# Sliding-window attention inside an MLP, one core: the scores and PVs of two head pairs issued as one group from batch 2 on

## The chip, the core and the metric

The kernel runs on one core of a Trainium2 chip. The metric is the device time of one execution in microseconds (us); the number compared is the median over several executions.

The engines have short names here, as in the profile: PE is TensorE (matmuls; PEld is its weight load), ACT is ScalarE, DVE is VectorE, POOL is GpSimd, SP is SyncE, which here only issues DMAs ("SPq" is its queue, "ACTq" is ACT issuing a DMA). Matmuls write to PSUM, which has eight banks; ACT and DVE read PSUM and write to SBUF.

## What is computed

Cut to what matters, the reference is:

```python
# q, k, v: [8 batches, 8 heads, 576 positions, 64]; w_in: [512, 2048]; w_out: [2048, 512]
scores = q @ k.T / 8                      # per batch and head
mask   = (0 <= i - j) & (i - j < 64)      # each query sees itself and the 63 keys before it
attn   = softmax(where(mask, scores, -1e9))
x      = (attn @ v), heads side by side   # [4608 tokens, 512]
h      = x @ w_in
out    = (h * clip(h + 3, 0, 6) / 6) @ w_out
```

The inputs are float32 and the kernel computes in bf16 with float32 accumulation. Most of the arithmetic is in the two products with `w_in` and `w_out`; the attention only needs a band of 64 keys per query.

## The kernel before

**The two-product part.** The 4608 tokens are cut into nine blocks T of 512. For each block, `s1(T)` (L747) computes the hidden layer in eight chunks c of 2 x 128 features: each chunk is eight matmuls of 512 columns (L767) into one PSUM slot, a RELU by ACT (L776) and a multiply by DVE (L779), which frees the slot and writes `gT`. Then `s2(T)` (L787) multiplies `gT` by `w_out`: 4 x 16 matmuls of 512 columns (L815), numbered n = 0 to 63, into two accumulator banks; after every 16th, `finish` (L825) has ACT copy the result to SBUF (L832) and SP store it (L837).

**The attention part** of batch b = T + 1 is woven into `s2(T)`, because `s1(T + 1)` needs its result. Eight heads are four pairs g. One pair's work is a unit "S" (scores) and a unit "PV":

- From batch 2 on (`NR6 = 2`), S is `scores64` (L637). A head's 576 queries are nine blocks i of 64. For each block and each head h of the pair, one matmul (L648) multiplies the block's 64 queries by a window of 128 keys (`kwin`, L627); it uses half of the PE's rows. Two parts, of five and four blocks, go to a PSUM slot each; ACT takes the exponential of a slot in one instruction (`ex`, L654), into the tile `pT`, 1152 columns per pair; after the second part DVE multiplies all of them by a 0/1 mask in place (`msk`, L658).
- PV is `pv64` (L665): 20 matmuls (L672) with `pT` as weights and V (or its copy shifted by 64 keys, `W`) as moving operand, half of the PE's columns each, into one PSUM slot. A column of ones in V gives the sums of the softmax. Then `norm` (L708) on DVE takes the reciprocals (L710) and multiplies (L713) into `opg`, and `xdma` (L717) has SP issue a DMA transpose of `opg` into `xT` (L720), the input of `s1`.

**What these wait for.** The queries and keys of a batch come in by SP (L455, ten DMAs a batch), are cast by POOL (`nat`, L277), and are transposed into `QKT` by two DMA transposes on SP's queue (L434, four pairs each). There is one `QKT` buffer (`NQT = 1`), so the next batch's transposes follow this batch's last scores. V comes in by DMAs that ACT issues (L381) and is cast by POOL. A ring of four tiles `P_ring` (`NPT = 4`, L193) holds `pT`; a pair takes tile (4b + g) mod 4.

**PSUM.** From `s2(0)` on there are three slots of two banks each and two accumulator banks. `two_banks` (L160) gives out the slot that comes free first and waits until its readers are done: a chunk's multiply, a part's exponential, or a pair's `norm`.

**The order of the work** is fixed when the program is built. `Plan` (L36) keeps a time of its own for the PE (`pl.t`), with a cost for each step; every operation of another engine has a due time and a cost, and on each engine they are put in order of due time (`pop`, L59). So the planner's costs decide the order in an engine's queue, and on the chip each queue is then worked off in that order. Where the attention units stand among the 64 matmuls of `s2` is written by hand: `REST` (L879) lists pairs of (n, unit). For batches 2 to 7, before: S of pair 0 ahead of matmul n = 4, S of pair 1 ahead of 10, S of pair 2 and PV of pair 0 ahead of 17, S of pair 3 and PV of pair 1 ahead of 23, PV of pair 2 ahead of 28, PV of pair 3 ahead of 33. Batches 0 and 1 use `FIRST`, `scores` and `pv128` (L573, L679).

Of the kernel before, what the change touches and what calls it, by code (L numbers as in the profile page):

```python
# [12 lines left out]
EXP = mybir.ActivationFunctionType.Exp  # L13
RELU = mybir.ActivationFunctionType.Relu
MULT = mybir.AluOpType.mult
# [7 lines left out]
NPT = 4  # L23
# [81 lines left out]
def kernel(  # L105
# [10 lines left out]
    P = nc.NUM_PARTITIONS  # L116
    B, H, S, D = q.shape
    DM, FF = moe_w_in.shape
    NT = B * S
    NG = H // 2  # L120
# [12 lines left out]
    scale = 1.0 / math.sqrt(D)  # L133
# [4 lines left out]
    pl = Plan()  # L138
# [15 lines left out]
    def free_at(i):  # L154
        return max((pl.done.get(r, 1e9) for r in held[i]), default=0.0)
# [4 lines left out]
    def two_banks(readers, dt=F32):  # L160
        i = min(range(len(psums)), key=free_at)
        while free_at(i) >= 1e9:
            pl.pop()
            i = min(range(len(psums)), key=free_at)
        for r in held[i]:
            pl.wait(r)
        held[i] = readers
        return psums[i].tile([P, 2, 512 if dt == F32 else 1024], dt, name=f"ps{i}", tag="ps")
# [10 lines left out]
    mask = consts.tile([P, QW], BF16, name="mask")  # L179
# [9 lines left out]
    def qk(b, i, g):  # L189

        return QK_tiles[b % NQT][:, 2 * g + i if b < NR6 else i * NG + g, :]

    P_ring = [consts.tile([P, 2, KB, 2 * P], BF16, name=f"pT{i}") for i in range(NPT)]  # L193
    V_ring = [consts.tile([P, NG, KB, 2, VW], BF16, name=f"V{i}") for i in range(2)]
    runs_flat = runs_all[:].rearrange("p a b c d -> p (a b c d)")
    NV = NG * KB * 2 * VW
    W_ring = [runs_flat[:, i * NV : (i + 1) * NV].rearrange("p (g k h w) -> p g k h w", g=NG, k=KB, h=2) for i in range(2)]
    BL = S // D

    mask64 = consts.tile([P, D], BF16, name="mask64")  # L200
# [14 lines left out]
    for j, t in enumerate(P_ring):  # L215
        at("ACT", 1.9, 0.55, lambda t=t: nc.scalar.copy(
            out=t[:, :, 0 : KB - 1, QW : 2 * P], in_=idle[:].rearrange("p (h k w) -> p h k w", h=2, w=D)))
        at("DVE", 2.0, 0.1, lambda t=t: nc.vector.memset(t[:, :, KB - 1, D:QW], 1.0))

    def band(t, fill):  # L220
# [12 lines left out]
        out=neg[:, 0 : 2 * QW].rearrange("p (k w) -> p k w", k=2),  # L233
        in_=neg32[:].unsqueeze(1).to_broadcast([P, 2, QW]),
    ) and None, None, deps=("neg32",))
    pl.op("DVE", 4.4, 0.25, lambda s: nc.vector.tensor_copy(
        out=neg[:, 2 * QW : 2 * QW + D], in_=neg32[:, 0:D]) and None, "neg", deps=("neg32",))
# [5 lines left out]
        out=m64[:], in_=m64[:], pattern=[[1, D]], compare_op=ISGE, fill=0.0, base=D, channel_multiplier=-1))  # L243
    at("POOL", 17.4, 0.3, lambda: nc.gpsimd.affine_select(
        out=m64[:], in_=m64[:], pattern=[[-1, D]], compare_op=ISGE, fill=0.0, base=-1, channel_multiplier=1), "m64")
# [381 lines left out]
    def kwin(b, g, i, h):  # L627

        t = QK_tiles[b % NQT]
        c = (2 * g + 1 if b < NR6 else NG + g) * SP + (i - 1) * D  # L630
        return t[:].rearrange("p a s -> p (a s)")[h * D : (h + 1) * D, c : c + P]

    def blocks(b, g):
        n = b * NG + g
        return P_ring[n % NPT][:].rearrange("p h k w -> p (h k w)")[:, 0 : 2 * S].rearrange("p (h c) -> p h c", h=2)

    def scores64(b, g):  # L637

        for i in range(2):
            pl.wait(("tr", b, i))  # L640
        QT, pT = qk(b, 0, g), blocks(b, g)
        for part in range(2):
            i0, i1 = ((0, 5), (5, BL))[part]
            st = two_banks([("exp", b, g, part)])
            for i in range(i0, i1):
                for h in range(2):
                    c = (i - i0) * D
                    nc.tensor.matmul(  # L648
                        st[:, h, c : c + D], lhsT=kwin(b, g, i, h), rhs=QT[h * D : (h + 1) * D, i * D : (i + 1) * D],
                        start=True, stop=True,  # L650
                    )
            pl.pe((0.25, 0.22)[part])
            def ex(s, st=st, i0=i0, i1=i1):
                nc.scalar.activation(  # L654
                    out=pT[:, :, i0 * D : i1 * D], in_=st[:, :, 0 : (i1 - i0) * D], func=EXP, scale=scale,
                )
            def msk(t):
                pl.op("DVE", t, 0.8, lambda s: nc.vector.tensor_tensor(  # L658
                    out=pT.rearrange("p h (i w) -> p (h i) w", w=D), in0=pT.rearrange("p h (i w) -> p (h i) w", w=D),
                    in1=mask64[:].unsqueeze(1).to_broadcast([P, 2 * BL, D]), op=MULT,  # L660
                ) and None, ("mask", b, g), deps=("mask64",))
            pl.op("ACT", pl.t + 0.1, (0.8, 0.69)[part], ex, ("exp", b, g, part), msk if part else None)
        pl.mark(("S", b, g), pl.t)

    def pv64(b, g, o):  # L665

        V, W, pT = V_ring[b % 2], W_ring[b % 2], blocks(b, g)
        for h in range(2):
            for m in range(KB):
                for odd in range(2):  # L670
                    i = min(2 * m + odd, BL - 1)
                    nc.tensor.matmul(  # L672
                        o[odd * D : (odd + 1) * D, h, m * VW : (m + 1) * VW],
                        lhsT=pT[:, h, i * D : (i + 1) * D],
                        rhs=(V if i % 2 else W)[:, g, m, h, :], start=True, stop=True,
                    )
        pl.pe(0.5)
# [18 lines left out]
    def pv(b, g):  # L696
# [3 lines left out]
        if b >= NR6:  # L700
            pl.need(("w0", b % 2))
            pv64(b, g, o)
        else:
            pv128(b, g, o)
# [82 lines left out]
    def s2(T, side):  # L787

        side = list(side)
        if T == 0:  # L790
            order = [(ts, fc) for f0 in (0, 8, 12) for ts in (0, 1) for fc in range(f0, 8 if f0 == 0 else f0 + 4)]
            order += [(ts, fc) for ts in (2, 3) for fc in range(NFC)]
        else:
            order = [(ts, fc) for ts in range(TB // P) for fc in range(NFC)]
        last = T == NTB - 1
        order = [(ts, 0, DM, fc) for ts, fc in order if not last or ts < TB // P - 1]
        if last:
            order += [(TB // P - 1, c0, c1, fc) for c0, c1 in ((0, 3 * P), (3 * P, DM)) for fc in range(NFC)]
        accs = {}
        for n, (ts, c0, c1, fc) in enumerate(order):  # L800
            while side and side[0][0] <= n:
                at_, f, b, g = side[0]
                if b < NR6 and not ready(f, b, g):
                    break
                side.pop(0)
                unit(f, b, g)
            if fc == 0:
                nst = T * 4 + ts + (c0 > 0)
                if nst >= 2:
                    pl.wait(("acc", nst - 2))  # L810
                accs[ts] = acc_pool.tile([P, DM], F32, name="acc", tag="acc")[:]
            pl.wait(("g", T, fc // 2))
            if T == 0:
                pl.wait(("wout", fc // 4, (fc % 4) // 2))
            nc.tensor.matmul(  # L815
                accs[ts][:, c0:c1], lhsT=gT[:, fc, ts * P : (ts + 1) * P], rhs=wout16[:, fc, c0:c1],
                start=(fc == 0), stop=(fc == NFC - 1),
            )
            pl.pe(0.216 * (c1 - c0) / DM)
            if fc == NFC - 1:  # L820
                finish(T, ts, accs[ts], c0, c1)
        for _, f, b, g in side:
            unit(f, b, g)
# [31 lines left out]
    def unit(f, b, g):  # L855
        if f == "T":
            tqk(b, g)
        elif f[0] == "S":
            if b < NR6:
                scores(b, g, (0, 1) if f == "S" else (int(f[1]),))  # L860
            else:
                scores64(b, g)
        elif f == "PV":
            cells[b, g] = pv(b, g)
        else:
            xt(b, g, cells.pop((b, g)))
# [4 lines left out]
    for r in held.pop():  # L871
# [4 lines left out]
    FIRST = ((6, "T", 0), (12, "T", 1), (16, "S", 0), (18, "S", 1), (0, "T", 2), (0, "T", 3),  # L876
             (0, "S", 2), (0, "S", 3), (0, "PV", 0), (0, "PV", 1), (0, "X", 0), (0, "PV", 2),
             (0, "X", 1), (0, "PV", 3), (0, "X", 2), (0, "X", 3))
    REST = ((4, "S", 0), (10, "S", 1), (17, "S", 2), (17, "PV", 0), (23, "S", 3), (23, "PV", 1),  # L879
            (28, "PV", 2), (33, "PV", 3))  # L880
    for T in range(NTB):
        pl.mark(("s1", T), pl.t)
        pl.mark(("s1v", T), pl.t + 0.2)
# [1 line left out]
        b = T + 1  # L885
        side = []
        if b < B:
            side = [(n, f, b, g) for n, f, g in (FIRST if b < NR6 else REST)]
        s2(T, side)
# [32 lines left out]
```

The softmax here doesn't subtract the row's maximum and nothing guards it: scores larger than these inputs give would overflow.

## Time and profile before

| what | value |
|---|---|
| median of 5 executions | 311.36 us (310.25 to 312.52) |
| the profiled execution | 312.86 us |
| its span, first to last instruction | 311.1 us |
| granted PE clock | 1.00 throughout |
| ACT, DVE, POOL busy | 157.4, 161.0, 116.6 us |
| start of `s2(T)` on the PE, T = 1 to 6 | 75.22, 108.30, 139.95, 171.44, 203.27, 234.92 us |
| from there to `s1(T + 1)`, T = 1 to 6 | 18.97, 17.68, 17.68, 17.68, 17.68, 17.68 us |
| `s2(7)`, which has no attention in it | 13.81 us |

The profiled execution took 312.86 us, of which 311.1 are the span and 1.8 lie around it; it is 1.5 us above the median. All starts are counted from the span's first instruction. "Busy" time counts a matmul's whole duration, and matmuls overlap, so it says little of how close the PE is to its limit; the starts of successive matmuls say more. Issue instructions on SP's queue have a start and an end too; a DMA lands later.

### The profile page before, as it was taken

What the parts mean: (1) busy time and instruction counts of PE and PEld (TensorE: products, weight loads), DVE (VectorE), ACT (ScalarE), POOL (GpSimd) and SP (SyncE); (2) the same over time, 40 slices, a digit from 0 to 9 for tenths busy, and PEclk for the clock granted to TensorE, in tenths of its full rate; (3) what the DMA queues carried; (4) which work ended last, traced back from release to release, by engine and by line L of the source; (5) the groups of instructions that cost most, each with busy time, mean ns of one, the idle gap of its engine ahead of it and who ended that gap; (6) DMA issues with size and microseconds to landing.
All of it is one profiled execution on the core that took longest, in us unless ns stands there. A gap on an engine that the chain in (4) does not pass through costs nothing.

```text
span 311.1 us, 6664 instructions
## 1 busy us (share of the span) xinstructions
PE 296.4 (95%) x2746; PEld 153.6 (49%) x2787; DVE 161.0 (52%) x208; ACT 157.4 (51%) x199; POOL 116.6 (37%) x185
## 2 busy tenths in 40 slices
PE   7989889998999999999999999999999999999996
PEld 2554345643544454785444444445575444444443
DVE  5576476757533774366426742666176616404610
ACT  5846488355615671467246623672458236315611
POOL 3257548527833742286227632573243000000000
PEclk9999999999999999999999999999999999999999
DMA  8999998999999998999899989999990520010011
GB/s 226 245 364 389 388 295 179 220 223 262 213 185 248 263 200 160 216 262 209 169 194 261 206 173 177 251 209 169 193 244 20 129 86 0 33 70 35 0 67 70
DMA packets 153487, 58.38 MB, mean 188 GB/s; under 512 B 142064, under 2 KB 143344, under 8 KB 153456
## 3 DMA queue, kind: packets, MB, share of 16 engines
q1 hardware_dynamic: 125184, 50.80, 75.9%
q10 hardware_dynamic: 28272, 7.15, 11.7%
q8 instruction: 22, 0.36, 0.5%
q14 instruction: 9, 0.07, 0.1%
HBM read 36.70 MB, written 9.44 MB: 148 GB/s over the span
## 4 chain that ended last, share of the span: by engine, by line
PE 69%; DMA 20%; SPq 3%; ACT 2%; DVE 2%; issue 2%; POOL 1%; ACTq 0%
PE acc L815 33%; PE ps L767 28%; DMA QKT<-nat 6%; DMA st<-in_moe_w_out_dram 5%; DMA st<-in_q_dram 4%; DMA st<-in_k_dram 4%; PE ps L672 3%; PE ps L648 3%; DMA xT<-opg 1%; SPq L837 1%; PE ps L562 1%; DMA st<-in_v_dram 1%; ACT pT L602 1%; SPq L455 1%; SPq L329 1%
## 5 line engine op out<-in xcount | busy, mean ns | idle before, releaser
L779 DVE SCALAR_TENSOR_TENSOR gT<-t,ps 128x1024 bf16<-128x1024 bf16 x72 | 87.7, 1221 | 101.5 <-ACT t L776 101.5
L815 PE MATMUL acc<-wout,gT 128*128 128x512 bf16 (+2 forms) x559 | 129.4, 373 | 3.7 <-issue 2.2
L767 PE MATMUL ps<-xT,win 128*128 128x512 bf16 (+4 forms) x696 | 126.1, 340 | 0.7 <-DVE gT L779 0.2
L776 ACT ACTIVATE t<-ps,half 128x1024 bf16<-128x1024 f32 x72 | 80.0, 1114 | 49.4 <-PE ps L767 47.6
L767 PEld LDWEIGHTS <-win 128*128 128x128 bf16 x704 | 65.2, 98 | 60.1 <-issue 1.0
L815 PEld LDWEIGHTS <-gT 128*128 128x128 bf16 x592 | 53.6, 98 | 58.7 <-issue 1.0
L832 ACT COPY osb<-acc 128x512 f32<-128x512 f32 (+2 forms) x37 | 21.3, 575 | 75.9 <-PE acc L815 72.3
L277 POOL CAST runs<-st 64x512 bf16<-64x512 f32 (+1 forms) x49 | 30.7, 627 | 64.8 <-DMA st<-in_v_dram 54.6
L277 POOL CAST nat<-st 128x512 bf16<-128x512 f32 x48 | 32.7, 688 | 23.9 <-DMA st<-in_k_dram 15.2
L654 ACT ACTIVATE pT<-ps 128x640 bf16<-128x640 f32 (+1 forms) x48 | 28.7, 650 | 10.8 <-PE ps L648 10.8
L713 DVE TENSOR_TENSOR opg<-ps,rec 128x640 bf16<-128x640 f32 x32 | 26.4, 824 | 1.1
L658 DVE TENSOR_TENSOR pT<-pT,mask 128x1152 bf16<-128x1152 bf16 x24 | 20.0, 832 | 7.3 <-ACT pT L654 7.3
L277 POOL CAST V<-st 128x512 bf16<-128x512 f32 (+1 forms) x30 | 18.8, 629 | 3.3 <-DMA st<-in_v_dram 1.7
L648 PEld LDWEIGHTS <-QKT 64*128 64x128 bf16 x432 | 7.6, 95 | 11.5 <-issue 9.8
L602 ACT ACTIVATE pT<-ps 128x768 bf16<-128x768 f32 x16 | 12.6, 823 | 0.8 <-PE ps L593 0.6
L672 PEld LDWEIGHTS <-pT 128*64 128x64 bf16 x480 | 9.5, 111 | 5.7 <-DVE opg L713 2.1
L672 PE MATMUL ps<-runs,pT 128*64 128x65 bf16 x288 | 12.2, 197 | 0.0
L648 PE MATMUL ps<-QKT 64*128 64x64 bf16 x432 | 10.5, 191 | 1.5 <-DMA QKT<-nat 1.2
L710 DVE RECIPROCAL rec<-ps 128x10 f32<-128x10 f32 x32 | 7.0, 217 | 9.5 <-PE ps L672 7.9
L274 DVE CAST runs<-st 128x576 bf16<-128x576 f32 x14 | 7.2, 519 | 9.0 <-DMA st<-in_q_dram 6.5
L276 ACT COPY QKT<-ps 128x1152 bf16<-128x1152 bf16 x8 | 9.0, 1120 | 5.5 <-PE ps L562 5.5
L672 PE MATMUL ps<-V,pT 128*64 128x65 bf16 x192 | 11.3, 198 | 0.0
(60 smaller groups left out, 118.6 us busy)
## 6 DMA issues: line engine op xcount, KB each, us to landing
out_dram<-osb SPq DMA_DIRECT2D x35, 256.0 KB, 3.5
st<-in_q_dram SPq DMA_DIRECT2D x24, 256.0 KB, 6.1
st<-in_k_dram SPq DMA_DIRECT2D x24, 256.0 KB, 5.4
st<-in_v_dram ACTq DMA_DIRECT2D x24, 256.0 KB, 5.3
st<-in_moe_w_out_dram SPq DMA_DIRECT2D x4, 1024.0 KB, 13.9
st<-in_moe_w_in_dram SPq DMA_DIRECT2D x3, 1024.0 KB, 10.9
st<-in_q_dram SPq DMA_DIRECT2D x8, 288.0 KB, 6.8
st<-in_k_dram SPq DMA_DIRECT2D x8, 288.0 KB, 6.9
```

What stands on the lines that cost most here:

```text
L277: return lambda s: nc.gpsimd.tensor_copy(out=out_ap, in_=in_ap) and None
L602: nc.scalar.activation(out=pT[:, :, kbs[0] : kbs[0] + 2, 0:QW], in_=st[:, :, 0 : 2 * QW].rearrange("p h (k w) -> p h k w", k=2), func=EXP, ...
L648: nc.tensor.matmul(st[:, h, c : c + D], lhsT=kwin(b, g, i, h), rhs=QT[h * D : (h + 1) * D, i * D : (i + 1) * D], start=True, stop=True,)
L654: nc.scalar.activation(out=pT[:, :, i0 * D : i1 * D], in_=st[:, :, 0 : (i1 - i0) * D], func=EXP, scale=scale,)
L658: pl.op("DVE", t, 0.8, lambda s: nc.vector.tensor_tensor(out=pT.rearrange("p h (i w) -> p (h i) w", w=D), in0=pT.rearrange("p h (i w) -> p ...
L672: nc.tensor.matmul(o[odd * D : (odd + 1) * D, h, m * VW : (m + 1) * VW], lhsT=pT[:, h, i * D : (i + 1) * D], rhs=(V if i % 2 else W)[:, g, ...
L713: nc.vector.tensor_tensor(out=opg[:].rearrange("p k h d -> p h k d"), in0=ov[:, :, :, 0:D], in1=rec[:].unsqueeze(3).to_broadcast([P, 2, KB ...
L767: nc.tensor.matmul(hT[:, j, dst : dst + w], lhsT=win16[:, g, (2 * c + j) * P : (2 * c + j + 1) * P], rhs=xT[:, g, src : src + w], start=(g ...
L776: nc.scalar.activation(out=t1[:], in_=hT[:], func=RELU, bias=half[:], scale=1.0 / 6.0)
L779: nc.vector.scalar_tensor_tensor(out=gT[:, 2 * c : 2 * c + 2, :], in0=cell["t"][:], scalar=1.0, in1=hT[:], op0=MIN, op1=MULT,)
L815: nc.tensor.matmul(accs[ts][:, c0:c1], lhsT=gT[:, fc, ts * P : (ts + 1) * P], rhs=wout16[:, fc, c0:c1], start=(fc == 0), stop=(fc == NFC - 1),
L832: nc.scalar.copy(out=osb[:, c0:c1], in_=acc[:, c0:c1])
```

## The change

`scores64` is now called for two pairs at once (gg = 0 for pairs 0 and 1, gg = 1 for pairs 2 and 3). Its 18 blocks are spread over three PSUM slots of six blocks, in order, so the second slot holds the last three blocks of the first pair and the first three of the second. There are three exponentials of 2 x 384 columns, and after the second and the third a mask multiply for one pair. Both pairs share one tile of `P_ring`, taken as (2b + gg) mod 4; `halves` hands each pair's part to `pv64`. `REST` now has S of pairs 0 and 1 ahead of n = 11, S of pairs 2 and 3 ahead of 18, both PVs of the first two pairs ahead of 25 and both of the last two ahead of 35. The planner's cost of an exponential of the new size is 0.82, of a mask multiply still 0.8.

```diff
-    def blocks(b, g):
-        n = b * NG + g
-        return P_ring[n % NPT][:].rearrange("p h k w -> p (h k w)")[:, 0 : 2 * S].rearrange("p (h c) -> p h c", h=2)
-
-    def scores64(b, g):
+    halves = {}
+    NB = 6
+
+    def scores64(b, gg):
 
         for i in range(2):
             pl.wait(("tr", b, i))
-        QT, pT = qk(b, 0, g), blocks(b, g)
-        for part in range(2):
-            i0, i1 = ((0, 5), (5, BL))[part]
-            st = two_banks([("exp", b, g, part)])
-            for i in range(i0, i1):
+        pT = P_ring[(b * 2 + gg) % NPT][:].rearrange("p h k w -> p (h k w)")[:, 0 : 4 * S].rearrange("p (h c) -> p h c", h=2)
+        todo = [(2 * gg + a, i) for a in range(2) for i in range(BL)]
+        for part in range(3):
+            st = two_banks([("exp", b, gg, part)])
+            for c, (g, i) in enumerate(todo[part * NB : part * NB + NB]):
                 for h in range(2):
-                    c = (i - i0) * D
                     nc.tensor.matmul(
-                        st[:, h, c : c + D], lhsT=kwin(b, g, i, h), rhs=QT[h * D : (h + 1) * D, i * D : (i + 1) * D],
-                        start=True, stop=True,
-                    )
-            pl.pe((0.25, 0.22)[part])
-            def ex(s, st=st, i0=i0, i1=i1):
+                        st[:, h, c * D : (c + 1) * D], lhsT=kwin(b, g, i, h),
+                        rhs=qk(b, 0, g)[h * D : (h + 1) * D, i * D : (i + 1) * D], start=True, stop=True,
+                    )
+            pl.pe(0.27)
+            def ex(s, st=st, part=part):
                 nc.scalar.activation(
-                    out=pT[:, :, i0 * D : i1 * D], in_=st[:, :, 0 : (i1 - i0) * D], func=EXP, scale=scale,
+                    out=pT[:, :, part * NB * D : (part + 1) * NB * D], in_=st[:, :, 0 : NB * D], func=EXP, scale=scale,
                 )
-            def msk(t):
+            def msk(t, a=part - 1):
+                P_half = pT[:, :, a * S : (a + 1) * S].rearrange("p h (i w) -> p h i w", w=D)
                 pl.op("DVE", t, 0.8, lambda s: nc.vector.tensor_tensor(
-                    out=pT.rearrange("p h (i w) -> p (h i) w", w=D), in0=pT.rearrange("p h (i w) -> p (h i) w", w=D),
-                    in1=mask64[:].unsqueeze(1).to_broadcast([P, 2 * BL, D]), op=MULT,
-                ) and None, ("mask", b, g), deps=("mask64",))
-            pl.op("ACT", pl.t + 0.1, (0.8, 0.69)[part], ex, ("exp", b, g, part), msk if part else None)
-        pl.mark(("S", b, g), pl.t)
+                    out=P_half, in0=P_half,
+                    in1=mask64[:].unsqueeze(1).unsqueeze(1).to_broadcast([P, 2, BL, D]), op=MULT,
+                ) and None, ("mask", b, 2 * gg + a), deps=("mask64",))
+            pl.op("ACT", pl.t + 0.1, 0.82, ex, ("exp", b, gg, part), msk if part else None)
+        for a in range(2):
+            halves[b, 2 * gg + a] = pT[:, :, a * S : (a + 1) * S]
+            pl.mark(("S", b, 2 * gg + a), pl.t)
 
     def pv64(b, g, o):
 
-        V, W, pT = V_ring[b % 2], W_ring[b % 2], blocks(b, g)
+        V, W, pT = V_ring[b % 2], W_ring[b % 2], halves.pop((b, g))
...
-    REST = ((4, "S", 0), (10, "S", 1), (17, "S", 2), (17, "PV", 0), (23, "S", 3), (23, "PV", 1),
-            (28, "PV", 2), (33, "PV", 3))
+    REST = ((11, "S", 0), (18, "S", 1), (25, "PV", 0), (25, "PV", 1), (35, "PV", 2), (35, "PV", 3))
```

## The prediction

> **What bounds the kernel now.** I read the page first, then the chain of work that ended last in order of time, the groups with shapes kept apart, the waits, and the timelines of ACT, DVE and SP.
>
> The page says which engine is never idle:
>
> ```profile
> PE 296.4 (95%) x2746; PEld 153.6 (49%) x2787; DVE 161.0 (52%) x208; ACT 157.4 (51%) x199; POOL 116.6 (37%) x185
> ```
>
> The chain in order of time, inside `s2(2)`, start and duration:
>
> ```profile
> 108.46 0.86 PE acc L815 x4
> 109.33 0.37 PE ps L648 x18
> 109.70 1.40 PE acc L815 x6
> ...
> 113.08 0.37 PE ps L648 x18
> 113.45 0.44 PE ps L672 x20
> 113.89 1.19 PE acc L815 x5
> ```
>
> From T = 2 on almost the whole chain is PE. A run of 512-column matmuls steps by 0.216 us; six of them would take 1.30, but take 1.40 with the way into S: from the last one's start to the first score is 0.31, so 0.095 is lost on the way in. Of S's 0.37, 0.25 lie between its first and last start (17 steps of 0.0145) and 0.12 are the way out; of PV's 0.44, 0.315 (19 steps of 0.0164) and 0.125. The way out costs the same from S to PV. So 17.68 - 13.81 = 3.87 us of attention per batch are 4 x 0.37 + 4 x 0.44 + 6 x 0.095 = 3.8.
>
> One wait of the PE on a transfer stands in the waits, at 77.47, the first scores of batch 2:
>
> ```profile
> PEld L648 <- DMA QKT<-nat: 1.7, 1, 1.7
> ```
>
> SP's queue in `s2(1)` (start, duration; xT<-opg are the four transposes of `opg`):
>
> ```profile
> 85.46 1.21 SPq L455 DMA_DIRECT2D tl<-in_k_dram  x1
> 86.77 0.56 SPq L837 DMA_DIRECT2D out_dram<-osb  x1
> 87.43 4.18 SPq L720 DMA_TRANSPOSE xT<-opg  x3
> 91.71 0.54 SPq L837 DMA_DIRECT2D out_dram<-osb  x1
> 92.34 1.23 SPq L720 DMA_TRANSPOSE xT<-opg  x1
> ```
>
> There is no pause in it: ten loads before, then these. The third transpose lands at 94.80, the fourth at 95.74, while `s1(2)` starts at 94.19 and stops for both. SP is a second bound, close behind the PE. The last transpose lands ahead of its use by 0.4, 3.9, 1.4, 0.4, 2.2 us for T = 2 to 6.
>
> **PE: fewer, longer groups.** Two S groups of 36 matmuls take 35 x 0.0145 + 0.12 = 0.63 each, two PV groups of 40 take 39 x 0.0164 + 0.125 = 0.77, four ways in 0.38: 3.17 for 3.79, a saving of 0.62 per batch, 3.7 for six. A changed slot inside a group costs nothing: the fifth block's step to the second slot is no longer than the others. The Trainium skill ("TensorEngine Tiling (Array Packing)", Key Properties) says that a change of tiling mode drains the array; mode changes fall from 14 to 8 per batch (S to PV counts), and with the 175 ns that "TensorE: Matmul & The Clock Gate" (Single matmul latency) gives for a drain the saving would be 6 x 0.175 = 1.05, an estimate. The trace shows about 0.1 for each way in or out, so I take 0.62; bounds 0.4 and 1.05.
>
> **ACT.** From the groups:
>
> ```profile
> L654 ACT ACTIVATE pT<-ps 128x640 bf16<-128x640 f32 x24 | 16.9, 706 | 10.8 <-PE ps L648 10.8
> L654 ACT ACTIVATE pT<-ps 128x512 bf16<-128x512 f32 x24 | 14.3, 594 | 0.0
> L602 ACT ACTIVATE pT<-ps 128x768 bf16<-128x768 f32 x16 | 12.6, 823 | 0.8 <-PE ps L593 0.6
> L658 DVE TENSOR_TENSOR pT<-pT,mask 128x1152 bf16<-128x1152 bf16 x24 | 20.0, 832 | 7.3 <-ACT pT L654 7.3
> ```
>
> The new size has a row, 823 ns, but in a row they start 0.71 apart (two take 1.42 at 50.47 in the chain), a copy 0.48. Let s be the first score of pairs 0 and 1, at n = 11: start of `s2` + 10 x 0.216 + 0.31 = + 2.47. The first exponential starts at s + 0.39 (last matmul of its slot + 0.23, as now), the next at 1.10 and 1.81; the third ends at 2.63. The copy of the first accumulator (due before the next exponentials) starts at 2.52, then come 3.00, 3.71, 4.42, the last two ending at 4.53 and 5.24. ACT does 6 x 0.71 = 4.3 us per batch where it did 4 x 1.19 = 4.8; neither is on the path.
>
> **The wait for the third slot.** S of pairs 2 and 3 starts at s + 0.63 + 6 x 0.216 + 0.31 = 2.24; its third slot is due at 2.59 but free at 2.63 + 0.05: the PE stalls 0.1, with all of `s2` behind it. Bounds: 0, and 0.3 if the exponentials start 0.82 apart. The first group's third slot is that of the last hidden chunk, freed at + 2.57 of `s2` (DVE at 110.87), before s + 0.35: nothing.
>
> **The last mask.** The DVE timeline shows the steps in its queue:
>
> ```profile
> 116.14 0.22 DVE L710 RECIPROCAL rec<-ps 128x10 f32<-128x10 f32 x1 [0.32 <-PE ps L672]
> 116.40 0.82 DVE L713 TENSOR_TENSOR opg<-ps,rec 128x640 bf16<-128x640 f32 x1
> 117.14 1.17 DVE L658 TENSOR_TENSOR pT<-pT,mask 128x1152 bf16<-128x1152 bf16 x1
> 118.23 0.21 DVE L710 RECIPROCAL rec<-ps 128x10 f32<-128x10 f32 x1
> ```
>
> A `norm` holds DVE for 1.00, a mask for 0.76 without POOL beside it. The order follows the planner's dues, counted from its own s: the mask of pair 2 at 5.21, `norm` of pair 0 at 5.33, of pair 1 at 5.83, the mask of pair 3 at 6.03 (exponentials 0.82 each, the copy 0.62 among them). So the last mask is queued behind two norms. On the chip: PVs 0 and 1 start at 2.24 + 0.63 + 0.10 + 1.61 = 4.58 and end at 5.35, their slots free at 3.82 and 4.58; DVE masks pair 2 at 4.57, norms from 5.33 and 6.33, masks pair 3 from 7.33 to 8.16. PV 2 starts at 5.35 + 9 x 0.216 + 0.31 = 7.60, PV 3 is due at 7.93 and waits until 8.21: 0.3 us in which the PE stands, and the 29 matmuls behind it. Now all masks are done before their PV. Lower bound 0. Upper bound 0.9: of the 24 masks before, seven took 0.89 to 1.17 us. The Trainium skill ("SBUF — State Buffer", Who interferes with whom) says why this speaks against the change: a DVE instruction with two SBUF inputs shares a port with GpSimd, one blocking the other whole; a cast of 0.69 us (L277) would make a mask 1.45, an estimate, and PV 3 would wait 1.5 if both masks were hit. No row exceeds 1.17, so I keep 0.9. The mask's new shape costs nothing: the three-dimensional one of the first batches (L614) takes 1086 ns for 1536 columns, 0.71 ns each, and this one 832 for 1152, 0.72. A `pT` tile now comes back after two batches instead of one, so nothing waits for it. The two pairs share a `pT` tile with interleaved columns; a wait drawn by whole tile would hold PV 2 too, but the casts of V, interleaved the same way, show none for each other.
>
> Net per batch: - 0.62 + 0.10 + 0.31 = - 0.21.
>
> **Scores of batch 2.** `QKT` lands at 77.43; the first score now stands at 75.22 + 2.47 = 77.69, so the stall there (1.30, from 76.17 to 77.47) is gone. But what is late next is SP: its loads hold it until 86.67, and the four transposes cannot come sooner; `s1(2)` would start at 94.19 - 1.30 - 0.21 = 92.7 and wait for the same landings at 94.80 and 95.74. The chunk ends where it did: gain 0, bounds 0 and - 1.5.
>
> **Transposes of the other batches.** `opg` of pair 0 is done at s + 6.4, + 8.9 of `s2`, where it was 6.7; of pair 3 at 12.65 for 12.3. With 1.3 per transpose and 0.6 per store the fourth is issued at about + 13.6 (now 12.5 to 14.3) and lands 2.6 to 4.6 later, by 18.2; it is needed at about + 18.8. No stall, by a margin of 0.6 at worst.
>
> **Sum.** 5 x (- 0.21) = - 1.05 for T = 2 to 6, nothing for T = 1. Against the profiled execution (312.86, span 311.1) that is 311.8; against the median of 311.36, 310.3. About 0.5% (1.56 us) is what a measurement here can tell from no change, so this lies inside it.
>
> **Rivals.**
> - *SP or DMA sets the period (chance 0.22): 311.2.* For: SP has no pause in T = 1 and 4, and the margins of 0.4 in T = 2 and 5 are small; then every gain of the PE is waited away at the next `s1`. Against: in T = 3 SP waits for a store at 153.71 to 154.99, so it follows the PE there.
> - *The last mask comes in time, and part of the T = 1 stall stays gone (0.24): 308.3.* 5 x (- 0.52) = - 2.6, and - 0.5 of the 1.5. For: stall and margin are a third of a microsecond; against: the order of the dues is fixed. With everything kept it is 307.
> - *The late `opg` becomes the stall (0.16): 313.6, slower.* The transposes run back to back from + 8.9 with two stores among them. One issue took 2.47 (at 119.33); with such a one and the longest landing the fourth lands at + 19.4, 0.6 to 0.8 after its use; with the - 0.21 that is + 0.45 for each of five batches, + 2.3. It decides once the fourth lands later than + 19.0.
>
> The case above has 0.38. Below 309.8 lie most of the second rival and a part of the first case (0.36); above 312.9 most of the third (0.16). The range of 308.0 to 312.8 leaves out the fully kept gain and the bad transposes.
>
> **What would show it.** Runs of 36 and 40 matmuls with about 3.2 us of their own; no wait of the PE on `QKT`; a wait of PV on a DVE mask of about 0.3 in each batch, and of S on an exponential of 0.1; `s2` of 17.4 to 17.5 us for T = 2 to 6; `s1(2)` stopping for `xT` by about 2 us. Wrong: if PV waits over 0.9, if `s1` waits for `xT` after T = 1, or if the start of `s2(2)` is over 0.7 earlier than 108.30.

## The result, and the profile after

Timed beside the kernel before, the changed kernel has a ratio of 0.9986 with a 95% interval of 0.9967 to 1.0006 (medians over all executions 312.33 and 312.02 us; the ratio leaves disturbed executions out, and two profiles below, of the PVs sooner and of the second try with V later, are of such executions). Timed once more on another occasion it has 0.9963 (0.9932 to 0.9993). So the change brings 0.4 to 1.2 us, at the edge of what can be told from nothing. The forecast of 310.3 was a gain of 1.05 us; the first comparison gives 0.44, less than half of that.

The profiled execution took 310.57 us, its span is 308.8. That is 2.3 less than in the profile of before, but 2.55 us of the difference are already there at the start of `s2(1)` (72.67 instead of 75.22), ahead of the first changed instruction: the first 75 us differ from execution to execution. What follows therefore compares distances inside a profile, not times from the start.

PE and ACT on the page: ACT has 12 instructions fewer.

```profile
PE 294.7 (95%) x2748; PEld 153.7 (50%) x2787; DVE 161.5 (52%) x208; ACT 154.6 (50%) x187; POOL 117.2 (38%) x185
```

The waits of the PE, longest first (us in total, times, longest):

```profile
PE ps L768 <- DMA xT<-opg: 2.4, 2, 1.3
...
PE ps L673 <- DVE pT L657: 0.9, 2, 0.5
```

Line 768 is `s1`, 673 is PV, 657 the mask. The wait on `QKT` that stood here before is gone. In its place are the two that the prediction named: `s1` stops for the transposes, and PV for a mask. In stages (start of one to start of the next, us):

| stage | before | before, second profile | changed | changed, second profile |
|---|---|---|---|---|
| `s2(1)` | 18.97 | 19.00 | 17.59 | 17.37 |
| `s1(2)` | 14.11 | 14.29 | 16.79 | 17.69 |
| start of `s2(1)` to start of `s2(2)` | 33.09 | 33.29 | 34.38 | 35.06 |
| `s2(2)` to `s2(6)`, mean | 17.68 | 17.68 | 17.38 | 17.28 |
| start of `s2(2)` to the end | 202.84 | 202.51 | 201.79 | 201.09 |

From the start of `s2(2)` on, the change gains about what was forecast, 0.7 to 1.8 us (forecast 1.05). In T = 1 it loses 1.1 to 2.0, where the forecast had nothing. One sign of being wrong that the prediction named did appear: `s2(2)` starts at 107.05, more than 0.7 ahead of 108.30. But that is the earlier start of `s2(1)`; counted from there it comes 1.3 later than before.

DVE in `s2(2)`, start and duration, shows the queue of which the prediction spoke:

```profile
115.14 0.21 DVE L711 RECIPROCAL rec<-ps 128x10 f32<-128x10 f32 x1
115.38 0.82 DVE L714 TENSOR_TENSOR opg<-ps,rec 128x640 bf16<-128x640 f32 x1
116.12 0.21 DVE L711 RECIPROCAL rec<-ps 128x10 f32<-128x10 f32 x1
116.36 0.82 DVE L714 TENSOR_TENSOR opg<-ps,rec 128x640 bf16<-128x640 f32 x1
117.10 0.98 DVE L657 TENSOR_TENSOR pT<-pT,mask 128x1152 bf16<-128x1152 bf16 x1
```

Two norms stand ahead of the mask of pair 3. It ends at 118.08, and the PE's weight load of PV 3 starts at 118.14:

```profile
117.10 0.40 PEld L673 LDWEIGHTS <-pT 128*64 128x64 bf16 x20 [0.42 <-issue]
118.14 0.40 PEld L673 LDWEIGHTS <-pT 128*64 128x64 bf16 x20 [0.65 <-DVE pT L657]
```

This is the worst of the six batches (`s2(2)` took 17.80): the mask of pair 2 was stretched to 1.15 us and this one to 0.98.

The PE at the start of `s1(2)`:

```profile
90.27 0.38 PE L768 MATMUL ps<-xT,win 128*128 128x512 bf16 x1
91.93 1.54 PE L768 MATMUL ps<-xT,win 128*128 128x512 bf16 x5 [1.29 <-DMA xT<-opg]
94.54 12.68 PE L768 MATMUL ps<-xT,win 128*128 128x512 bf16 x57 [1.06 <-DMA xT<-opg]
```

It starts 1.4 us sooner after `s2(1)` began than before, and then stands until the second and the fourth transpose have landed.

### The profile page after: what moved, and what is told of

Read it like the earlier page. It is cut to its first block, busy times and chain, and to the rows that moved or that the text cites. A ratio compares the mean times of both kernels' runs of the same rounds, so it can differ in the third digit from the quotient of the medians.

```text
span 308.8 us, 6651 instructions
## 1 busy us (share of the span) xinstructions
PE 294.7 (95%) x2748; PEld 153.7 (50%) x2787; DVE 161.5 (52%) x208; ACT 154.6 (50%) x187; POOL 117.2 (38%) x185
## 4 chain that ended last, share of the span: by engine, by line
PE 61%; DMA 16%; SPq 7%; DVE 4%; ACT 4%; issue 3%; POOL 3%; ACTq 0%; POOLq 0%
PE ps L768 29%; PE acc L816 28%; DMA QKT<-nat 6%; DMA st<-in_moe_w_out_dram 5%; DMA st<-in_v_dram 5%; ACT pT L652 3%; SPq L354 2%; PE ps L673 2%; DVE opg L714 2%; SPq L329 2%; PE ps L646 2%; DVE pT L657 2%; SPq L721 1%; DMA xT<-opg 1%; SPq L412 1%
## 5 line engine op out<-in xcount | busy, mean ns | idle before, releaser
L816 PE MATMUL acc<-wout,gT 128*128 128x512 bf16 (+2 forms) x561 | 128.0, 373 | 2.8 <-issue 1.9
L816 PEld LDWEIGHTS <-gT 128*128 128x128 bf16 x592 | 54.5, 98 | 60.3
L277 POOL CAST nat<-st 128x512 bf16<-128x512 f32 x48 | 33.9, 712 | 20.4 <-DMA st<-in_k_dram 10.8
L652 ACT ACTIVATE pT<-ps 128x768 bf16<-128x768 f32 x36 | 26.9, 837 | 9.3 <-PE ps L646 9.3
L657 DVE TENSOR_TENSOR pT<-pT,mask 128x1152 bf16<-128x1152 bf16 x24 | 21.1, 895 | 16.0 <-ACT pT L652 16.0
L602 ACT ACTIVATE pT<-ps 128x768 bf16<-128x768 f32 x16 | 12.7, 833 | 0.9 <-PE ps L593 0.8
L673 PE MATMUL ps<-runs,pT 128*64 128x65 bf16 x288 | 11.0, 197 | 1.0 <-DVE pT L657 0.9
L673 PE MATMUL ps<-V,pT 128*64 128x65 bf16 x192 | 10.4, 198 | 0.0
L277 POOL CAST wout<-st 128x1024 bf16<-128x1024 f32 x6 | 7.4, 1251 | 6.0 <-DMA st<-in_moe_w_out_dram 6.0
L277 POOL CAST nat<-tl 64x512 bf16<-64x512 f32 x12 | 8.0, 669 | 2.8 <-DMA tl<-in_k_dram 1.6
## 6 DMA issues: line engine op xcount, KB each, us to landing
st<-in_moe_w_in_dram SPq DMA_DIRECT2D x3, 1024.0 KB, 10.3
```

The lines of the kernel that those rows point to most:

```text
L277: return lambda s: nc.gpsimd.tensor_copy(out=out_ap, in_=in_ap) and None
L602: nc.scalar.activation(out=pT[:, :, kbs[0] : kbs[0] + 2, 0:QW], in_=st[:, :, 0 : 2 * QW].rearrange("p h (k w) -> p h k w", k=2), func=EXP, ...
L652: nc.scalar.activation(out=pT[:, :, part * NB * D : (part + 1) * NB * D], in_=st[:, :, 0 : NB * D], func=EXP, scale=scale,)
L657: pl.op("DVE", t, 0.8, lambda s: nc.vector.tensor_tensor(out=P_half, in0=P_half, in1=mask64[:].unsqueeze(1).unsqueeze(1).to_broadcast([P, ...
L673: nc.tensor.matmul(o[odd * D : (odd + 1) * D, h, m * VW : (m + 1) * VW], lhsT=pT[:, h, i * D : (i + 1) * D], rhs=(V if i % 2 else W)[:, g, ...
L816: nc.tensor.matmul(accs[ts][:, c0:c1], lhsT=gT[:, fc, ts * P : (ts + 1) * P], rhs=wout16[:, fc, c0:c1], start=(fc == 0), stop=(fc == NFC - 1),
```

## The experiments

**Theory A** is the prediction's: the PE is the bound in T = 2 to 6, and in T = 1 SP's queue. **Theory B**, its first rival: SP and the DMA engines set the period everywhere, and what the PE saves is waited away.

**The changed kernel again** (no edit).

> The changed kernel once more, timed beside the kernel before on one chip. Theory A (the PE is the bound in T = 2 to 6, gains 0.62 us per batch by grouping and gives 0.1 and 0.3 back to the third slot and to the last mask; in T = 1 SP's queue is the bound and takes the gain): 1.0 us faster than before, ratio 0.997; s2 of 17.2 to 17.8 us for T = 2 to 6, PV groups of pairs 2 and 3 lasting 0.9 to 1.5 instead of 0.77, s1(2) of 15.5 to 17 us. Theory B (SP and the DMA engines set the period, the PE's savings are waited away): ratio 1.000, s1(T + 1) longer by what s2(T) is shorter, for every T.

Measured: ratio 0.9963 (0.9932 to 0.9993). `s2(2)` to `s2(6)` took 17.17 to 17.58. `s1(3)` to `s1(7)` took 13.97, 14.01, 14.20, 13.97 and 13.81, in sum 0.25 and 0.6 us more than in the two profiles of before. So they take back only a small part of the 2.0 us that the five `s2` save, which speaks against B. But `s1(2)` was 17.69, longer than expected.

**The last mask ahead of the second norm.**

```diff
-                pl.op("DVE", t, 0.8, lambda s: nc.vector.tensor_tensor(
+                pl.op("DVE", t - 0.3, 0.8, lambda s: nc.vector.tensor_tensor(
```

> One figure of the planner changed: the mask of each group's second pair is due 0.3 us earlier, so on DVE the last mask stands ahead of the norm of pair 1. Nothing else differs. Theory A: the wait of PV 3 on the mask is gone, PV groups of pairs 2 and 3 take 0.77 to 0.85 us, s2 is 16.9 to 17.2 for T = 2 to 6; 1.5 us faster than the changed kernel, 2.5 faster than before (ratio 0.992). Theory B: the groups shorten but s1(T + 1) waits for xT instead; the same as the changed kernel within 0.3 us.

Measured: ratio 0.9916 (0.9877 to 0.9954), median 310.48; `s2` took 17.07 or 17.08 in all six batches. On DVE the mask of pair 3 now stands between the norms:

```profile
114.95 0.21 DVE L711 RECIPROCAL rec<-ps 128x10 f32<-128x10 f32 x1
115.19 0.82 DVE L714 TENSOR_TENSOR opg<-ps,rec 128x640 bf16<-128x640 f32 x1
115.93 0.75 DVE L657 TENSOR_TENSOR pT<-pT,mask 128x1152 bf16<-128x1152 bf16 x1
116.60 0.21 DVE L711 RECIPROCAL rec<-ps 128x10 f32<-128x10 f32 x1
```

From the start of `s2(2)` to the end it is 199.93, against 201.79 and 201.09. Theory A holds: the PE's 0.2 to 0.3 us per batch count in full. The rest of the gain lies in T = 1, which takes 33.44 us from `s2(1)` to `s2(2)` in this profile, 0.9 to 1.6 less than in the two of the changed kernel; only 0.3 to 0.5 of that is in `s2(1)`, where the mask no longer delays the PV.

**The PVs of pairs 2 and 3 sooner**, the same wait made longer.

```diff
-... (35, "PV", 2), (35, "PV", 3))
+... (32, "PV", 2), (32, "PV", 3))
```

> The changed kernel with the PVs of pairs 2 and 3 ahead of n = 32 instead of 35. Theory A (PE and the order on DVE decide in T = 2 to 6): PV 3 comes 0.65 us sooner, the mask does not, so each s2 waits 0.5 to 0.65 longer, 17.8 to 18.0 for T = 2 to 6; 2.5 to 3 us slower than the changed kernel, ratio to before 1.005. Theory B (SP sets the period): the longer s2 is covered, s1 is shorter by as much, ratio as the changed kernel.

Measured: ratio 1.0042 (1.0020 to 1.0064); `s2(2)` to `s2(6)` 17.82 to 18.18, which is 0.75 to 1.1 longer than with the mask first, with 0.55 to 0.9 us of idle PE ahead of the last PV in each; `s1(3)` to `s1(7)` no shorter. With these two runs B falls for T = 2 to 6, in both directions.

**The PVs one by one**, the scores still grouped.

```diff
-... (25, "PV", 0), (25, "PV", 1), (35, "PV", 2), (35, "PV", 3))
+... (25, "PV", 0), (28, "PV", 1), (35, "PV", 2), (38, "PV", 3))
```

> The changed kernel with the PVs one by one again, ahead of n = 25, 28, 35 and 38; the scores stay grouped. Theory A: two more ways in and out, 0.40 us per batch, against a wait of 0.3 on the last mask that is now covered by three more matmuls (0.65): s2 of 17.2 to 17.4 for T = 2 to 6, equal to the changed kernel within 0.5 us, PV waits on the mask gone; T = 1 as with the change. Ratio to before 0.996 to 0.998. Theory B: s2 shorter or longer without effect, ratio 1.000.

Measured: ratio 0.9995 (0.9967 to 1.0023), less of a gain than A expected, though the interval reaches into its range; `s2` 17.52 or 17.53 in all six batches, 0.1 above the expected range. No PV waits for a mask. Against 17.07 with the mask first, two more groups cost 0.45 us (0.40 expected). So grouping the PVs, with the order on DVE that comes with it, is worth 0.15 to 0.25 us per batch; with the better order 0.45.

**What T = 1 costs: the change undone for batch 2 alone.** The old scores and old places for batch 2, the new ones for 3 to 7.

```diff
...
-    scores64(b, g)
+    (scores64_old if b == NR6 else scores64)(b, g)
...
-    side = [(n, f, b, g) for n, f, g in (FIRST if b < NR6 else REST)]
+    side = [(n, f, b, g) for n, f, g in (FIRST if b < NR6 else OLD if b == NR6 else REST)]
```

> The change undone for batch 2 alone (old scores, old places in s2(1)), kept for batches 3 to 7. Theories C and D both: T = 1 is as before, 33.1 us, and the gain of T = 2 to 6 stays (200.9 to 201.8 us from the start of s2(2) to the end instead of 202.8), so 1.0 to 1.5 us faster than the changed kernel, ratio to before 0.993 to 0.995. If T = 1 costs nothing, as the prediction had it: the same as the changed kernel.

Measured: ratio 0.9930 (0.9905 to 0.9956), median 310.09. Leaving batch 2 alone makes the changed kernel 0.3 to 0.6% faster, by the ratios: the change costs 1.0 to 1.8 us in T = 1. The prediction's "gain 0" falls. The profile shows less of it than expected: 33.90 from `s2(1)` to `s2(2)`, not 33.1. There `QKT` landed 0.3 us later after the start of `s2(1)` than in both profiles of before, a PV waited 0.3 us for a cast of V, and `s2(1)` took 19.73; `s1(2)`, with 14.17, is as before.

**The kernel before again**, for a second profile.

> The kernel before once more, for a second profile of T = 1. The changed kernel's two profiles have 34.4 and 35.1 us from the start of s2(1) to that of s2(2), against 33.1 in the one profile of before. If the change itself costs that time in T = 1, this profile has 32.8 to 33.5 again, and its fourth transpose of opg lands about 9 us after the last load of keys left SP's queue (9.1 in the first profile, 10.3 and 11.3 with the change). If it is the execution that differs, it has 34 to 35 too.

Measured: 33.29, the fourth transpose 9.18 after the loads' end. So the loss comes with the change and not with one execution. But its size varies: kernels with the same two score groups in T = 1 have 33.44 (mask first) and 33.80 (PVs one by one).

**Why the transposes land later.** SP's queue in T = 1 of the changed kernel, and what ACT issues beside it:

```profile
83.16 1.05 SPq L455 DMA_DIRECT2D tl<-in_k_dram  x1
84.32 0.56 SPq L838 DMA_DIRECT2D out_dram<-osb  x1
84.98 1.29 SPq L721 DMA_TRANSPOSE xT<-opg  x1
86.37 0.53 SPq L838 DMA_DIRECT2D out_dram<-osb  x1
86.99 4.80 SPq L721 DMA_TRANSPOSE xT<-opg  x3
```

```profile
87.10 0.41 ACTq L381 DMA_DIRECT2D st<-in_v_dram  x1
90.53 0.39 ACTq L381 DMA_DIRECT2D st<-in_v_dram  x1
```

The same two loads of V before the change, where the loads of keys ended at 86.67:

```profile
91.02 0.39 ACTq L381 DMA_DIRECT2D st<-in_v_dram  x1
94.46 0.39 ACTq L381 DMA_DIRECT2D st<-in_v_dram  x1
```

With the change the loads of keys end at 84.21. ACT issues two loads of V (256 KB each) 2.9 and 6.3 us later; before, they came 4.4 and 7.8 us after the loads. They follow the copies of accumulators on ACT's queue, so a PE that is 1.5 us ahead issues them 1.5 us sooner, while SP is where it was. And the second store stands ahead of the second transpose, since `opg` is due later in the plan. Theory C: the loads of V share the DMA engines with the transposes. Theory D: the store in the middle does it.

*V later, first try.* The first load of V behind the copy of the last accumulator.

```diff
-        pl.op("ACT", 0.0, 0.45, issue(0), deps=deps + tdeps)
+        if b == NR6 + 1:
+            pl.op("hold", 0.0, 0.2, lambda s: None, ("vhold", b), deps=deps + tdeps)
+            pl.op("ACT", 0.0, 0.45, issue(0), deps=(("vhold", b),))
+        else:
+            pl.op("ACT", 0.0, 0.45, issue(0), deps=deps + tdeps)
```

> The changed kernel with one thing moved: in T = 1 the first load of V that ACT issues stands behind the copy of the last accumulator, not ahead of it, so it leaves about 3.4 us later and the second one after it. Theory C (in T = 1 the earlier PE lets ACT issue loads of V while SP's transposes of opg are still on the DMA engines, and they share them): the fourth transpose lands 9 us after the last load of keys instead of 10.3 to 11.3, start of s2(1) to start of s2(2) is 33.3 instead of 34.4 to 35.1; 1.0 us faster than the changed kernel, ratio to before 0.993. Theory D (the transposes are late because opg itself is later and a store now stands ahead of the second one): nothing changes, 34.4 to 35.1.

Measured: ratio 1.0131 (1.0082 to 1.0180), slower, against both theories. The last load of V on ACT's queue now waited until 107.32 for POOL's casts, with a RELU of `s1(2)` behind it, and the PE stood 2.07 us for what follows from that RELU. Before that it had stood 2.60 us for a transpose, and from 95.9 to 99.3 its granted clock was 0.50. So `s1(2)` took 21.74. The first transpose happened to take 2.84 us to issue, and the fourth landed 10.3 us after the loads. It decides nothing between C and D; it shows that ACT's queue carries `s1`.

*V later, second try.* The last load is moved behind the RELUs as well.

```diff
...
-                    pl.op("ACT", s + (VGAP2 if b == NR6 else VGAP), 0.45, issue(kb + 1))
+                    pl.op("ACT", s + (VGAP2 if b == NR6 else VGAP + (4.0 if (b, kb) == (NR6 + 1, KB - 2) else 0.0)), 0.45, issue(kb + 1))
...
```

> The changed kernel with, in T = 1 alone, the first two loads of V that ACT issues each one place later (the first behind the copy of the last accumulator, the second behind two RELUs) and the last, of the tail, behind all RELUs, so that ACT is not held by it. Nothing else differs. Theory C (loads of V, issued earlier because the PE is earlier, share the DMA engines with the last transposes of opg): the fourth transpose lands 9.0 to 9.6 us after the end of the last load of keys instead of 10.3 to 11.3, s2(1) to s2(2) 33.3, 1.0 us faster than the changed kernel, ratio to before 0.993. Theory D (the order on SP's queue: a store now stands ahead of the second transpose): 34.4 to 35.1 as with the change, ratio 0.997.

Measured: ratio 1.0014 (0.9989 to 1.0039). The fourth transpose lands 8.92 after the loads, and from `s2(1)` to `s2(2)` it is 31.96, shorter than in any other kernel whose transposes are on SP, though the store still stands ahead of the second transpose. So far C, with a reservation: in this profile the loads also ended 10.45 us after the start of `s2(1)`, sooner than in the two of the changed kernel (11.54 and 11.18). And the time is given back at once. POOL's cast of the last part of V now stands behind six casts of queries and keys, at 116.31 (105.50 in the changed kernel), and PV in `s2(2)` waits for it for 4.2 us. Right after that, from 117.3 to 120.7, the granted clock is 0.50. So `s2(2)` takes 23.05 instead of 17.4. In the waits from 105 to 130 us (total, times, longest; L677 is PV in this kernel, `runs` holds the shifted copy of V):

```profile
PE ps L677 <- POOL runs L277: 4.2, 1, 4.2
```

*The store last.*

```diff
-            pl.op("SP", t, 0.1, fn, ("st", nst))
+            pl.op("SP", t + (5.0 if (T, ts) == (1, 1) else 0.0), 0.1, fn, ("st", nst))
```

> The changed kernel with, in T = 1 alone, the store of the second accumulator behind the four transposes on SP's queue, not between the first and the second. Theory D: the transposes are issued without a pause, the fourth 5.2 us after the loads' end instead of 6.3, and lands about 9 after it; s2(1) to s2(2) 33.3, ratio to before 0.993. Theory C: the store's own 0.6 us of issue is saved and no more, the fourth lands 9.7 to 10.5 after the loads, s2(1) to s2(2) 34.0, ratio 0.995.

Measured: ratio 0.9978 (0.9952 to 1.0005). The fourth transpose lands 8.05 after the loads, sooner than D expected, and from `s2(1)` to `s2(2)` it is 33.2, as D had it; the total is not better than the changed kernel's. The chain of this run shows what is late next:

```profile
92.29 7.94 DMA QKT<-nat
100.23 0.02 issue
100.25 0.37 ACTq L381
...
100.73 1.12 ACT t L777
101.85 0.02 issue
101.88 1.23 DVE gT L780
103.11 0.04 issue
103.15 3.61 PE ps L768 x16
```

A load of V on ACT's queue is held until the transposes into `QKT` have landed at 100.23; behind it stand a RELU, then DVE, then a slot, and the PE waits 1.0 us.

The runs side by side, us after the end of the last load of keys:

| kernel | 256 KB transfers issued by then | fourth transpose issued | landed |
|---|---|---|---|
| before, two profiles | 3 | 5.7, 5.7 | 9.1, 9.2 |
| change undone for batch 2 | 3 | 5.8 | 9.2 |
| PVs one by one | 3 | 5.4 | 9.8 |
| last mask first | 3 | 5.4 | by 10.1 (first use; no record) |
| V later, first try | 3 | 7.0 | 10.3 |
| changed, two profiles | 4 (the last within 0.2 of it) | 6.4, 6.3 | 10.3, 11.3 |
| PVs of pairs 2 and 3 sooner | 4 | 6.4 | 10.4 |
| V later, second try | 2 | 6.2 | 8.9 |
| store last | 2 | 5.4 | 8.1 |

Moving loads of V and moving the store each brought the landing forward, so C and D are both parts of it, as far as one profile of each can show. From its issue to its landing the fourth transpose takes 2.6 and 2.7 us with two such transfers, 3.3 to 3.5 with three (4.4 in the PVs one by one) and 3.9 to 5.1 with four. The rest is the time of issue, which has causes of its own: where the last load of keys takes 2.1 us to issue instead of 1.1 (PVs one by one, mask first, first try), the count starts 1 us later. The runs do not separate how much is each one's.

**The x of batch 2 transposed by the PE**, so that `s1(2)` needs nothing from SP.

```diff
-        ... None if b < NXP else xdma,
+        ... None if b <= NXP else xdma,
...
+    REST2 = REST[:4] + ((35, "PV", 2), (35, "X", 0), (35, "X", 1), (42, "PV", 3), (42, "X", 2), (52, "X", 3))
...
```

> The changed kernel, but the x of batch 2 is transposed by the PE, as it is for batches 0 and 1, and not by four DMA transposes on SP's queue; its units stand between the PVs of s2(1). Theory A (the gain of T = 1 is lost because s1(2) waits for those four transposes): s1(2) falls from 16.8 us (14.1 before) to 13.8, s2(1) grows by four groups of five transposes at about 0.5 us each, 2.0 in all; start of s2(1) to start of s2(2) is 33.4 instead of 34.4; 1.0 us faster than the changed kernel, ratio to before 0.994. Theory B (SP sets the period): SP is relieved of some 5 us in T = 1 and everything after comes earlier by 3 to 5 us, ratio 0.985.

Measured: ratio 0.9904 (0.9875 to 0.9933), median 308.70. `s1(2)` is 13.81 with no wait, `s2(1)` is 18.41, and from `s2(1)` to `s2(2)` it is 32.23, 2.2 to 2.8 less than with the change. That is more than A expected, because the twenty transposes cost 1.1 us and not 2.0, and less than B.

**Both**, the mask first and the x of batch 2 by the PE.

> The last mask ahead of the norm of pair 1, and the x of batch 2 transposed by the PE, together. Theory A: the two gains lie in different stages and add: 2.5 us faster than the changed kernel, 3.5 faster than before (ratio 0.989). Theory B: as with the PE transposes alone.

Measured: ratio 0.9863 (0.9823 to 0.9904), median 307.31: the fastest of all, better than both kernels. `s2(1)` to `s2(2)` 32.35, `s2(2)` to the end 199.42.

## Why the prediction was right for T = 2 to 6 and wrong for T = 1

- *PE, fewer and longer groups, - 0.62 per batch:* right. With no mask in the way `s2` is 17.07 for 17.68, 0.61 less, with 0.06 of slot wait still in it. Had each change of mode cost the drain of about 175 ns that the Trainium skill names within the latency of one matmul ("TensorE: Matmul & The Clock Gate", Single matmul latency), it would have been 1.05, by the prediction's estimate; the measurement sides with the row.
- *The third slot, + 0.10:* right in kind, 0.06: the second score group spreads its first and last starts by 0.57 us, the first by 0.51.
- *The last mask, + 0.31:* right. `s2(2)` to `s2(6)` are 0.31 and 0.21 longer on average than with the mask first; the worst batch had 0.73, inside the bound of 0.9. That POOL stretches a mask was there too (0.98 to 1.15 in that batch, a mean of 895 ns for 832 before; in both profiles no mask without a POOL instruction beside it took more than 0.76, and several with one took no more either); the wait of 1.5 that the port rule of the Trainium skill ("SBUF — State Buffer", Who interferes with whom) would allow was not seen.
- *Transposes of the other batches, no stall:* right; after T = 1 no wait of `s1` on `xT` stands in the waits, and `s1(3)` to `s1(7)` are as in the first profile of before, within 0.25 us.
- *The rival "SP sets the period":* wrong for T = 2 to 6, as two runs show; the late `opg` did not become a stall there either.
- *"Scores of batch 2 ... The chunk ends where it did: gain 0, bounds 0 and - 1.5":* this is the step that failed. It held the landings of 94.80 and 95.74 fixed, as if only SP's loads set them, and it gave no bound on the side of a loss. The transposes are also set by what else is on the DMA engines. The PE's own gain brought the loads of V forward by 1.5 us, the plan put a store between, and the fourth transpose landed 1.1 to 2.2 us later, counted from the loads' end, so that T = 1 took 34.4 and 35.1 us instead of 33.1 and 33.3. Undoing the change there is worth 0.3 to 0.6%, and taking `s1(2)` off these transposes brings it to 13.81.

One thing beside the wait differs, and no run tested it: the granted clock. It was below 0.997 in 28 of the 58 executions of the changed kernel on record, in 19 of the 132 of the kernel before that were timed beside these runs, and in 4 of 22 with the change undone for batch 2. In three profiles (PVs sooner, and both tries with V later) a stretch of 3.4 us at half the clock lies within about 1 us of the end of a stop of the PE. The page of the first try shows it as one slice of 40:

```profile
PEclk9999999999997999999999999999999999999999
```

Where the PE is the bound such a stretch costs up to 1.7 us, half its length, by estimate. Among executions at 0.997 and above, the second timing has a median of 310.5 us for the changed kernel beside 312.2 for the kernel before, and the timing with batch 2 undone has 309.9 beside 312.1. That leaves about 0.5 us between the two kernels. So part of what T = 1 costs in the timed runs may be a clock that falls more often, with the longer stop of the PE as the likely reason; how much is open.

So the sum had - 1.05 for T = 2 to 6, where the profiles show - 0.7 to - 1.8, and nothing for T = 1, where they show + 1.1 to + 2.0. That the two first profiles give just - 1.05 from the start of `s2(2)` on is in part luck: `s2` gained 0.30 and 0.40 per batch, not 0.21, and `s1(3)` to `s1(7)` took 0.25 to 0.8 us of that back. Taken together the change would bring about nothing, and 0.4 to 1.2 us of gain were measured; with profiles that differ by 0.7 us among themselves, that remainder is not resolved.

## What to carry to other kernels

A stage that a transfer ends gives back the time that you save ahead of it, and it can take more: look not only at whether the transfer's own queue is full, but at which other transfers your faster engine will issue earlier into the same DMA engines. And when a change lengthens a group on one engine, count the order in the next engine's queue: two norms ahead of one mask cost a third to a half of what the grouping gained (0.2 to 0.3 of 0.6 us per batch), and moving one due time by 0.3 us brought it back.

## What the runs showed of the hardware that was not expected

- Moving the first two loads of V behind the transposes, or one store, brought the landing of a DMA transpose of 640 columns forward by 1.4 to 3.3 us, in one profile of each.
- A load on ACT's queue is as much on the path as SP's transposes: held until 100.23 by the transposes into `QKT`, or until 107.32 by a cast, it left ACT idle for 2.6 and 3.7 us ahead of the next RELU, and the PE then stood for 1.0 and 2.1 us.
- Twenty 128 x 128 transposes on the PE, woven into `s2(1)`, cost about 1.1 us in all, about 0.055 each, by the starts around them.
- The granted clock halved for 3.4 us close to the end of a stop of the PE in three profiles (stops of 1.1, 2.6 and 4.2 us); other profiles have stops of 1.1 to 1.7 us without it.
